# Constant bias in a logarithm, pointer constants in small softmax operations, and the first loads in another order: attention with a rational feed-forward on one core

## The chip, the cores and the metric

One NeuronCore of a Trainium2 chip runs the whole kernel as one program. The metric is the device time of one execution in microseconds; the times given for the kernel before are three runs, and a profile was taken of one further execution. Engines are named as the profile names them: PE (TensorE, with PEld for its weight loads), DVE (VectorE), ACT (ScalarE), POOL (GpSimd) and SP (SyncE, which issues every load and store).

## The reference

Two attentions and a feed-forward layer, on 8 batches of 8 heads, 576 rows of 64 columns:

```
p_packed = softmax(p k^T / 8) v            # 32 packed queries per head
out      = softmax(q p_packed^T / 8) p_packed
x = out as 4608 rows of 512
h = x @ w_in                               # 512 x 2048
g = (a0 + a1 h + a2 h^2 + a3 h^3) / (1 + |b0||h| + |b1| h^2 + 1e-6)
y = g @ w_out                              # 2048 x 512
```

Each softmax divides by its sum plus 1e-9. The weights `w_in` and `w_out` arrive as 64-bit floats and are turned into 32-bit floats on the chip.

## The kernel before

**The work.** The feed-forward is cut into 128 *units*: one batch, one half of its 576 rows, one chunk of 256 of the 2048 hidden columns (`hidden`, L882 on). A unit multiplies on PE into a PSUM tile `h`; ACT makes `U` = |b0 h|, `sq` = b1 h^2 and the first term of the polynomial `Y` from it; DVE continues `Y`; POOL adds `U` and `sq`; ACT takes the logarithm of that sum plus one (`sq<-U,one`, the operation at L905) and the exponential of its negative, which is the reciprocal that divides; two DVE operations finish. Three units later `acc_block` multiplies the result by `w_out` into `acc`. The first 12 units (`PLAIN`) multiply in full 32-bit precision; from the 13th on each operand is split into a high and a low part (`split`, `divide`), with a cast on ACT (`gh`, `half`, `w`) and a subtraction on POOL (`gl`, `w<-w,w 128x512`).

**Weights.** `load_words` loads the 64-bit words in 16 pairs of transfers of 512 KB, in the order in which they fall due: `w_in` chunks 0 to 3 are pairs 1 to 4, `w_out` chunks 0, 1 and 2 are pairs 5, 6 and 7, and pair 8 is `w_in` chunk 4. A pair waits for a free buffer: `m` buffers, or the ring `w`, of which buffers 2 and 3 hold v and q of batch 0 until that attention is done (`started`). `convert` turns a pair into 32-bit floats: two ACT operations of 128x1024 (`w<-w`, `m<-m`, `half<-w`, `win<-w`), two on DVE and a sum on DVE or POOL. `divide` splits a chunk of `w_out` (one cast on ACT, two subtractions of 128x512 on POOL).

**Attention.** `attention(bb)` of batch 0 runs ahead of everything; that of each later batch is spread between the units of the batch before. Its small operations work on a tile `small`: the negated row maximum (128x2, or 128x1 with a pointer), `tot` = sum + 1e-9 (128x2), and in the second softmax a sum + 1e-9 of 128x18.

**The order.** Every operation is recorded by a `Planner` with a cost; it builds the dependencies, simulates the engines with these costs and issues all engines in the order found. So the cost of one operation, or one more dependency, moves operations everywhere. Only the operations recorded before `nc.pin()` (L1005) keep their written order: the list of first loads at L1000. All other transfers, those of `a` and `b` among them (L404, recorded in `constants`), are placed by the planner. Each transfer also waits until the one eight places ahead of it has landed. In gaps of PE the planner's times leave, `idle` puts small products with a tile of zeros (`acc<-w,zero`).

Names in the rows are those of tiles (`kx`, `AH`: attention; `at`, `acc`, `h`: PSUM). All planned instructions have L293 as their line.

Of the kernel before, what the change touches and what calls it, by code (L numbers as in the profile page):

```python
# [13 lines left out]
F32 = mybir.dt.float32  # L14
# [10 lines left out]
P = 128  # L25
# [4 lines left out]
S = 2.0**-40  # L30


class Planner:
# [61 lines left out]
    def cost(self, engine, name, args, kwargs):  # L95
        if engine == "sync":
            return self.DMA_ISSUE
        fixed, per = self.COST[engine]
        if engine == "tensor":
            if name == "transpose" or args[1].dtype == F32:  # L100
                fixed, per = self.TRANSPOSE if name == "transpose" else self.F32
        aps = [x for x in args if isinstance(x, bass.AP)]
        if engine == "scalar":
            fixed += (aps[-1].space == PSUM) * -42 + ("accum_out" in kwargs) * 93 + ("bias" in kwargs) * 93
            per += 0.1 * any(x.ap[-1][0] == 2 for x in aps[:2])
        if engine == "gpsimd" and len(aps) < 3:
            fixed, per = 135, 0.9
        if engine == "vector" and len(aps) > 2 and any(self.columns(x) == 1 for x in aps[1:]):
            fixed += 60
        if engine == "vector" and name == "tensor_scalar":  # L110
            per /= 2
        return fixed + per * self.columns(aps[1] if name.startswith("reduce") else aps[0])
# [24 lines left out]
    def shares(self, engine, calls):  # L137
# [9 lines left out]
        wide = sum(self.columns(x) > 8 for x in aps[1:])  # L147
        return wide > 1 or name in ("tensor_scalar", "tensor_copy")

# [175 lines left out]
def attention_rational_ffn(  # L325
# [46 lines left out]
    make_identity(tc.nc, ident)  # L372
    ab, abS, one, root = (sb.tile([P, n], F32, name=x) for n, x in ((6, "ab"), (7, "abS"), (1, "one"), (5, "root")))
    zero = sb.tile([P, 32], F32R, name="zero")
# [26 lines left out]

    def constants():
        nc.vector.tensor_scalar(zero, ident[:, 0:32], 0.0, None, ALU.mult)
        nc.sync.dma_start(ab[:, 0:4], a.rearrange("(o n) -> o n", o=1).broadcast_to([P, 4]))  # L404
        nc.sync.dma_start(ab[:, 4:6], b.rearrange("(o n) -> o n", o=1).broadcast_to([P, 2]))
        nc.vector.tensor_scalar(abS[:, 0:6], ab, S, None, ALU.mult)
        nc.vector.scalar_tensor_tensor(abS[:, 4:6], abS[:, 4:6], -1.0, abS[:, 4:6], ALU.mult, ALU.max)
        nc.vector.memset(one, (1.0 + 1e-6) * S)

# [125 lines left out]
    def load(bb, what):  # L535
        if bb >= B:
            return
        if what == "rem":
# [83 lines left out]
    def attention(bb):  # L622
# [58 lines left out]
        for r in range(NG):  # L681
# [36 lines left out]
            for x in range(2):  # L718
                nc.vector.reduce_max(mx[:, 2 * x + r : 2 * x + r + 1], t[x], axis=AX.X)
            nc.vector.tensor_scalar(of(nb, r), of(mx, r), -SCALE, None, ALU.mult)  # L720
            for x, (c0, c1) in enumerate(KEYS):
# [9 lines left out]
        else:  # L731
            fs = sm
        nc.vector.scalar_tensor_tensor(tot, fs[:, 0:2], 1e-9, fs[:, 2:4], ALU.add, ALU.add)
        nc.vector.reciprocal(rec, tot)
# [98 lines left out]
        for r in range(NG):  # L833
# [6 lines left out]
            nc.vector.reduce_sum(m2[:, 1, :], sT, axis=AX.X)  # L840
            nc.vector.tensor_scalar(m2[:, 1, :], m2[:, 1, :], 1e-9, None, ALU.add)
            nc.vector.reciprocal(m2[:, 2, :], m2[:, 1, :])
# [39 lines left out]
    def hidden(bb, x, c):  # L882
# [21 lines left out]
        yield  # L904
        nc.scalar.activation(U2, U, AF.Ln, bias=one)  # L905
        nc.scalar.activation(V, U2, AF.Exp, scale=-1.0)
# [92 lines left out]

    for what in ("k0", "k1", "r", "p", "qr", 2, "rv", "v0", "v1", 3, "q0", "q1", 4, 5):  # L1000
        if isinstance(what, int):
            load_words(what)
        else:
            load(0, what)
# [113 lines left out]
```

## Time and profile before

| | |
|---|---|
| three runs | 767.41 us median (766.51 to 767.48) |
| the profiled execution | 767.14 us, span 765.4 us |
| mean granted clock of TensorE | 0.982 of full speed |
| busy share of the span | PE 97%, PEld 74%, DVE 86%, ACT 81%, POOL 61% |
| chain of waits, by engine | PE 84%, ACT 6%, DVE 3%, POOL 3%, issue 2%, DMA 1% |
| bytes moved | 56.39 MB |

The span is cut by what the chain of waits goes through: it says, going back from the last instruction, which engine's work each stretch ended on. PE's busy time is not PE at its peak, since matmuls are pipelined and their ends are modelled. Idle time of an engine that is not on the chain costs nothing by itself.

### The profile page before, as it was taken

Reading aid. Unit: us, or ns where it says so; the run is one execution under the profiler, and the core shown is the slowest. Engines: PE = TensorE matmul, PEld = TensorE weight load, DVE = VectorE, ACT = ScalarE, POOL = GpSimd, SP = SyncE. Lnnn points to the kernel's source line nnn. Section 1 sums busy time; section 2 is a strip of 40 time slices with the busy share of each in tenths; the row PEclk is TensorE's granted clock in tenths of the full one; section 3 lists DMA queues with packets and bytes.
Section 4 is the critical chain, followed back from the end, with each engine's and each line's share of the span. In section 5 each row is a group of like instructions: output and inputs, shape, how many; then the busy total and the mean of one; then the engine's idle time right before and its main releaser. Section 6 shows DMA issues by size and latency. Waiting matters only on the chain.

```text
span 765.4 us, 14423 instructions
## 1 busy us (share of the span) xinstructions
PE 738.8 (97%) x5325; PEld 566.5 (74%) x5325; DVE 658.5 (86%) x1042; ACT 619.6 (81%) x1074; POOL 467.0 (61%) x455
## 2 busy tenths in 40 slices
PE   4679999999999999999999999999999999999997
PEld 3456554678788788778788887778887888778886
DVE  2889999988999779998988879998999788988873
ACT  5689978988887787878786877888787797888882
POOL 0024548986686556756685565856687555866762
PEclk8679999999999999999999999999999999999999
DMA  8994740214701139025602119021901006000001
GB/s 261 293 366 126 199 92 0 63 56 60 107 1 56 43 38 127 2 85 68 99 1 57 37 32 141 2 84 25 118 17 56 28 17 91 1 28 1 28 1 42
DMA packets 156632, 56.39 MB, mean 74 GB/s; under 512 B 126865, under 2 KB 145809, under 8 KB 156561
## 3 DMA queue, kind: packets, MB, share of 16 engines
q1 hardware_dynamic: 156560, 55.46, 33.3%
q8 instruction: 42, 0.69, 0.4%
q14 instruction: 30, 0.24, 0.1%
HBM read 46.01 MB, written 9.44 MB: 72 GB/s over the span
## 4 chain that ended last, share of the span: by engine, by line
PE 84%; ACT 6%; DVE 3%; POOL 3%; issue 2%; DMA 1%; SPq 0%; DVEq 0%; POOLq 0%; ACTq 0%
PE acc L293 43%; PE h L293 25%; PE at L293 15%; DVE Y L293 1%; POOL w L293 1%; ACT sq L293 1%; POOL U L293 1%; ACT U L293 1%; ACT m L293 1%; ACT Y L293 1%; ACT kx L293 1%; POOL gl L293 1%; DVE small L293 1%; ACT w L293 1%; DMA pn<-in_p_dram 1%
## 5 line engine op out<-in xcount | busy, mean ns | idle before, releaser
L293 POOL TENSOR_TENSOR U<-U,sq 128x576 f32<-128x576 f32 x128 | 186.4, 1456 | 141.4 <-ACT sq L293 137.0
L293 DVE SCALAR_TENSOR_TENSOR Y<-Y,abS,h 128x576 f32<-128x576 f32 x256 | 205.8, 805 | 50.6 <-ACT h L293 48.6
L293 PE MATMUL acc<-w,gh 128*128 128x512 f32 x736 | 239.2, 408 | 0.4 <-ACT half L293 0.3
L293 PE MATMUL h<-AH,m 128*128 128x288 f32 x1024 | 194.6, 314 | 0.5 <-DVE Y L293 0.2
L293 POOL TENSOR_TENSOR gl<-Y,gh 128x512 fp32r<-128x512 f32 x116 | 150.2, 1295 | 57.7 <-POOL G L293 18.4
L293 PEld LDWEIGHTS h<-AH,m 128*128 128x128 f32 x1024 | 159.7, 189 | 28.9 <-issue 9.8
L293 PEld LDWEIGHTS acc<-w,gh 128*128 128x128 f32 x736 | 133.4, 188 | 42.5 <-issue 12.3
L293 PE MATMUL acc<-w,gl 128*128 128x512 f32 x384 | 152.7, 416 | 1.3 <-POOL gl L293 1.2
L293 ACT ACTIVATE sq<-U,one 128x576 f32<-128x576 f32 x128 | 100.8, 788 | 34.0 <-POOL U L293 33.4
L293 ACT ACTIVATE U<-h 128x576 f32<-128x576 f32 x128 | 83.4, 651 | 34.9 <-PE h L293 33.8
L293 DVE TENSOR_TENSOR Y<-Y,h 128x576 f32<-128x576 f32 x128 | 95.5, 746 | 14.8 <-ACT Y L293 13.5
L293 ACT ACTIVATE h<-sq 128x576 f32<-128x576 f32 x128 | 84.8, 663 | 18.5 <-DVE Y L293 15.8
L293 ACT ACTIVATE Y<-h,abS 128x576 f32<-128x576 f32 x128 | 96.3, 752 | 0.0
L293 DVE SCALAR_TENSOR_TENSOR h<-U,h 128x576 f32<-128x576 f32 x128 | 96.2, 751 | 0.0
L293 PE MATMUL h<-AL,m 128*128 128x288 f32 x448 | 95.8, 294 | 0.0
L293 PEld LDWEIGHTS acc<-w,gl 128*128 128x128 f32 x384 | 71.8, 188 | 29.3 <-issue 10.5
L293 DVE SCALAR_TENSOR_TENSOR Y<-h,Y 128x576 f32<-128x576 f32 x116 | 87.1, 751 | 1.8
L293 ACT CAST gh<-Y 128x512 fp32r<-128x512 f32 x116 | 72.5, 625 | 19.1 <-DVE Y L293 12.3
L293 ACT ACTIVATE sq<-h 128x576 f32<-128x576 f32 x128 | 83.4, 651 | 0.0
L293 PE MATMUL acc<-half,gh 128*128 128x512 f32 x240 | 79.3, 412 | 0.0
L293 PEld LDWEIGHTS h<-AL,m 128*128 128x128 f32 x448 | 71.8, 188 | 0.1
L293 PEld LDWEIGHTS acc<-half,gh 128*128 128x128 f32 x240 | 43.4, 188 | 13.7 <-issue 5.8
(144 smaller groups left out, 900.8 us busy)
## 6 DMA issues: line engine op xcount, KB each, us to landing
w<-in_moe_w_out_dram SPq DMA_DIRECT2D x16, 512.0 KB, 4.7
out_dram<-half SPq DMA_DIRECT2D x15, 512.0 KB, 3.1
nat<-in_k_dram SPq DMA_DIRECT2D x48, 144.0 KB, 4.1
nat<-in_q_dram SPq DMA_DIRECT2D x48, 144.0 KB, 4.3
nat<-in_v_dram SPq DMA_DIRECT2D x24, 256.0 KB, 3.4
m<-in_moe_w_in_dram SPq DMA_DIRECT2D x10, 512.0 KB, 8.9
w<-in_moe_w_in_dram SPq DMA_DIRECT2D x6, 512.0 KB, 9.2
nat<-in_k_dram SPq DMA_DIRECT2D x4, 512.0 KB, 6.8
```

Source lines behind the costliest of these rows:

```text
L293: getattr(getattr(self.nc, engine), name)(*args, **kwargs)
```

## The change

Five edits. The logarithm's bias is a number instead of a pointer to the one-column tile `one`, which goes. Two columns behind `a` and `b` hold 1e-9 and -1/8, set by POOL; the negated maximum of batches 0 and 1 and the 128x18 sum take their constant from there as a pointer, and `tot` becomes two operations of one column with a pointer. The loads of `a` and `b` go into the fixed list, ahead of q. Pairs 6 and 7 follow pair 5 in the fixed list, into `w` buffers that are free (before, the planner placed them, and they went into the buffers of v and q). The planner's costs follow: a number as bias costs nothing extra, and a `tensor_scalar` with a pointer counts as one column a cycle and as not sharing POOL's port.

```diff
--- before.py
+++ after.py
@@ -101,13 +101,13 @@
                 fixed, per = self.TRANSPOSE if name == "transpose" else self.F32
         aps = [x for x in args if isinstance(x, bass.AP)]
         if engine == "scalar":
-            fixed += (aps[-1].space == PSUM) * -42 + ("accum_out" in kwargs) * 93 + ("bias" in kwargs) * 93
+            fixed += (aps[-1].space == PSUM) * -42 + ("accum_out" in kwargs) * 93 + isinstance(kwargs.get("bias"), bass.AP) * 93
             per += 0.1 * any(x.ap[-1][0] == 2 for x in aps[:2])
         if engine == "gpsimd" and len(aps) < 3:
             fixed, per = 135, 0.9
         if engine == "vector" and len(aps) > 2 and any(self.columns(x) == 1 for x in aps[1:]):
             fixed += 60
-        if engine == "vector" and name == "tensor_scalar":
+        if engine == "vector" and name == "tensor_scalar" and len(aps) == 2:
             per /= 2
         return fixed + per * self.columns(aps[1] if name.startswith("reduce") else aps[0])
 
@@ -145,7 +145,7 @@
         if any(x.space == PSUM for x in aps):
             return False
         wide = sum(self.columns(x) > 8 for x in aps[1:])
-        return wide > 1 or name in ("tensor_scalar", "tensor_copy")
+        return wide > 1 or name in ("tensor_scalar", "tensor_copy") and len(aps) == 2
 
     def mode(self, engine, calls):
 
@@ -370,7 +370,8 @@
 
     ident = sb.tile([P, P], F32, name="ident")
     make_identity(tc.nc, ident)
-    ab, abS, one, root = (sb.tile([P, n], F32, name=x) for n, x in ((6, "ab"), (7, "abS"), (1, "one"), (5, "root")))
+    ab, abS, root = (sb.tile([P, n], F32, name=x) for n, x in ((8, "ab"), (7, "abS"), (5, "root")))
+    ab, eps, minus = ab[:, 0:6], ab[:, 6:7], ab[:, 7:8]
     zero = sb.tile([P, 32], F32R, name="zero")
     win = sb.tile([P, NCH, NCC, CF], F32, name="win")
     G = sb.tile([P, NFC, 2 * REM], F32, name="G")
@@ -400,12 +401,11 @@
 
 
     def constants():
+        nc.gpsimd.memset(eps, 1e-9)
+        nc.gpsimd.memset(minus, -SCALE)
         nc.vector.tensor_scalar(zero, ident[:, 0:32], 0.0, None, ALU.mult)
-        nc.sync.dma_start(ab[:, 0:4], a.rearrange("(o n) -> o n", o=1).broadcast_to([P, 4]))
-        nc.sync.dma_start(ab[:, 4:6], b.rearrange("(o n) -> o n", o=1).broadcast_to([P, 2]))
         nc.vector.tensor_scalar(abS[:, 0:6], ab, S, None, ALU.mult)
         nc.vector.scalar_tensor_tensor(abS[:, 4:6], abS[:, 4:6], -1.0, abS[:, 4:6], ALU.mult, ALU.max)
-        nc.vector.memset(one, (1.0 + 1e-6) * S)
 
         m, e, p, r, i = (root[:, n : n + 1] for n in range(5))
         nc.vector.scalar_tensor_tensor(m, ab[:, 5:6], -1.0, ab[:, 5:6], ALU.mult, ALU.max)
@@ -534,6 +534,10 @@
 
     def load(bb, what):
         if bb >= B:
+            return
+        if what == "ab":
+            nc.sync.dma_start(ab[:, 0:4], a.rearrange("(o n) -> o n", o=1).broadcast_to([P, 4]))
+            nc.sync.dma_start(ab[:, 4:6], b.rearrange("(o n) -> o n", o=1).broadcast_to([P, 2]))
             return
         if what == "rem":
             for x in ("r", "p", "qr", "rv"):
@@ -717,7 +721,7 @@
             )
             for x in range(2):
                 nc.vector.reduce_max(mx[:, 2 * x + r : 2 * x + r + 1], t[x], axis=AX.X)
-            nc.vector.tensor_scalar(of(nb, r), of(mx, r), -SCALE, None, ALU.mult)
+            nc.vector.tensor_scalar(of(nb, r), of(mx, r), minus, None, ALU.mult)
             for x, (c0, c1) in enumerate(KEYS):
                 i = slice(2 * x + r, 2 * x + r + 1)
                 nc.scalar.activation(KX[:, r, c0:c1], t[x], AF.Exp, bias=nb[:, i], scale=SCALE, accum_out=sm[:, i])
@@ -730,7 +734,8 @@
             nc.vector.tensor_mul(fs, f, sm)
         else:
             fs = sm
-        nc.vector.scalar_tensor_tensor(tot, fs[:, 0:2], 1e-9, fs[:, 2:4], ALU.add, ALU.add)
+        for r in range(NG):
+            nc.vector.tensor_scalar(tot[:, r : r + 1], fs[:, r : r + 1], eps, fs[:, 2 + r : 3 + r], ALU.add, ALU.add)
         nc.vector.reciprocal(rec, tot)
         if rows4(bb):
             nc.vector.tensor_mul(xr(F), xr(f), two(rec))
@@ -838,7 +843,7 @@
             nc.scalar.activation(sT, sT, AF.Exp, scale=SCALE)
             yield
             nc.vector.reduce_sum(m2[:, 1, :], sT, axis=AX.X)
-            nc.vector.tensor_scalar(m2[:, 1, :], m2[:, 1, :], 1e-9, None, ALU.add)
+            nc.vector.tensor_scalar(m2[:, 1, :], m2[:, 1, :], eps, None, ALU.add)
             nc.vector.reciprocal(m2[:, 2, :], m2[:, 1, :])
             eng.tensor_mul(sT, sT, bc(2))
             if bb == 0:
@@ -902,7 +907,7 @@
         nc.vector.scalar_tensor_tensor(Y, Y, a1, V, ALU.add, ALU.mult)
         nc.gpsimd.tensor_add(U, U, U2)
         yield
-        nc.scalar.activation(U2, U, AF.Ln, bias=one)
+        nc.scalar.activation(U2, U, AF.Ln, bias=(1.0 + 1e-6) * S)
         nc.scalar.activation(V, U2, AF.Exp, scale=-1.0)
         nc.vector.scalar_tensor_tensor(Y, Y, a0, V, ALU.add, ALU.mult)
         nc.vector.scalar_tensor_tensor(V, U, (1.0 + 1e-6) * S, V, ALU.add, ALU.mult)
@@ -997,7 +1002,7 @@
         elif i == 1:
             nc.sync.dma_start(ov, o)
 
-    for what in ("k0", "k1", "r", "p", "qr", 2, "rv", "v0", "v1", 3, "q0", "q1", 4, 5):
+    for what in ("k0", "k1", "r", "p", "qr", 2, "rv", "v0", "v1", 3, "ab", "q0", "q1", 4, 5, 6, 7):
         if isinstance(what, int):
             load_words(what)
         else:
```

**The loads.** On SP's queue, from v of batch 0 on (`w_1`: v, `w_2`: q, `m_3`, `m_4`: pairs 3 and 4, `w_3`: pair 5; `nat`, `AH_2`, `pn_2`: batch 1), before:

```order
L293 DMA w_1_82<-in_v_dram 128x4x256 x2
L293 DMA m_3_83<-in_moe_w_in_dram 128x2x256 x2
L293 DMA w_2_84<-in_q_dram 128x4x256 x2
L293 DMA m_4_85<-in_moe_w_in_dram 128x2x256 x2
L293 DMA w_3_86<-in_moe_w_out_dram 128x512 x2
L293 DMA ab<-in_moe_b_dram 128x2
L293 DMA nat_3_106<-in_k_dram 128x4x256
L293 DMA ab<-in_moe_a_dram 128x4
L293 DMA AH_2_108<-in_k_dram 64x8x64
```

and now:

```order
L293 DMA w_1_81<-in_v_dram 128x4x256 x2
L293 DMA m_3_82<-in_moe_w_in_dram 128x2x256 x2
L293 DMA ab<-in_moe_a_dram 128x4
L293 DMA ab<-in_moe_b_dram 128x2
L293 DMA w_2_83<-in_q_dram 128x4x256 x2
L293 DMA m_4_84<-in_moe_w_in_dram 128x2x256 x2
L293 DMA w_3_85<-in_moe_w_out_dram 128x512 x2
L293 DMA w_4_86<-in_moe_w_out_dram 128x512 x2
L293 DMA w_5_87<-in_moe_w_out_dram 128x512 x2
L293 DMA nat_3_107<-in_k_dram 128x4x256
```

`a` and `b` stand ahead of q; pairs 6 and 7 (`w_4_86`, `w_5_87`) stand ahead of batch 1's k, where before they followed ten transfers of batch 1.

**ACT ahead of the first unit.** From the last copies of batch 0's first products (`m_7`) to the first unit's `U`, before:

```order
L293 COPY m_7_134<-at_17_135 128x256
L293 ACTIVATE root<-root 128x1
L293 COPY m_7_134<-at_18_136 128x256
L293 ACTIVATE root<-root 128x1
L293 TENSOR_LOAD abS x2
L293 ACTIVATE w_4_119<-w_4_119 128x1024
L293 TENSOR_LOAD abS
L293 COPY kx_2_141<-at_19_143 128x512
L293 COPY kx_2_141<-at_20_144 128x512
L293 ACTIVATE w_8_132<-w_4_119 128x1024
L293 ACTIVATE U_1_126<-h_1_127 128x576
```

and now:

```order
L293 COPY m_7_133<-at_17_134 128x256
L293 COPY m_7_133<-at_18_135 128x256
L293 ACTIVATE w_4_86<-w_4_86 128x1024
L293 ACTIVATE w_8_131<-w_4_86 128x1024
L293 ACTIVATE w_5_87<-w_5_87 128x1024
L293 ACTIVATE half_1_156<-w_5_87 128x1024
L293 COPY kx_2_140<-at_19_142 128x512
L293 COPY kx_2_140<-at_20_143 128x512
L293 ACTIVATE U_1_125<-h_1_126 128x576
```

The square root's operations (`root`) and the register loads from `abS` moved ahead; the conversion of pair 7 (`w_5`, `half_1`) moved in front of the first unit, beside that of pair 6 (`w_4`).

**POOL around the 9th to 14th unit.** `w_17` to `w_19` 128x512 are subtractions of `divide`, `U_9` and so on the units' sums; before:

```order
L293 TENSOR_TENSOR U_9_219<-U_9_219,sq_9_222 128x576
L293 TENSOR_TENSOR U_10_231<-U_10_231,sq_10_234 128x576
L293 TENSOR_TENSOR U_11_238<-U_11_238,sq_11_241 128x576
L293 TENSOR_TENSOR kx_2_141<-kx_2_141,small 128x576
L293 TENSOR_TENSOR w_17_254<-w_15_226,w_17_254 128x512
L293 TENSOR_TENSOR kx_2_141<-kx_2_141,small 128x576
L293 TENSOR_TENSOR U_12_250<-U_12_250,sq_12_253 128x576
L293 TENSOR_TENSOR w_17_254<-w_15_226,w_17_254 128x512
L293 TENSOR_TENSOR w_16_246<-w_14_215,w_16_246 128x1024
L293 TENSOR_TENSOR w_19_276<-w_16_246,w_19_276 128x512
```

and now:

```order
L293 TENSOR_TENSOR U_9_218<-U_9_218,sq_9_221 128x576
L293 TENSOR_TENSOR w_18_259<-w_15_225,w_18_259 128x512 x2
L293 TENSOR_TENSOR w_19_275<-w_16_245,w_19_275 128x512
L293 TENSOR_TENSOR U_10_230<-U_10_230,sq_10_233 128x576
L293 TENSOR_TENSOR kx_2_140<-kx_2_140,small 128x576
L293 TENSOR_TENSOR w_19_275<-w_16_245,w_19_275 128x512
L293 TENSOR_TENSOR kx_2_140<-kx_2_140,small 128x576
L293 TENSOR_TENSOR U_11_237<-U_11_237,sq_11_240 128x576
L293 TENSOR_TENSOR w_16_245<-w_14_198,w_16_245 128x1024
```

Four of the subtractions now stand ahead of `U_11`, where before none did (two others, `half_6`, stood between units 7 and 9 and now stand behind unit 2).

## Rows read from the trace of the kernel before

**Rows 1.** Busy time by stretch: start and end in us, length, then busy us (and instructions) of PE, PEld, DVE, ACT and POOL, the granted clock of TensorE, the busy share of the DMA engines, GB/s.

```profile
0.00:48.50 48.50, 28.34 (x301) 19.66 (x301) 30.85 (x70) 31.64 (x59) 4.59 (x11) 0.78 0.96 293
48.50:114.50 66.00, 65.93 (x441) 38.10 (x446) 62.22 (x97) 59.05 (x98) 29.36 (x16) 0.95 0.61 172
114.50:158.70 44.20, 43.09 (x255) 25.20 (x254) 42.69 (x70) 38.90 (x63) 40.51 (x35) 1.00 0.14 39
158.70:765.00 606.30, 601.39 (x4338) 483.58 (x4338) 522.75 (x809) 490.02 (x856) 392.50 (x395) 1.00 0.27 48
```

**Rows 2.** Pieces of the chain of waits: start in us, length in us, engine and tile written.

```profile
66.40 2.10 PE acc L290 x24
...
123.81 4.59 POOL w L293 x3
...
158.68 2.11 PE acc L293 x8
```

**Rows 3.** Shares of the chain by engine and tile in the stretch 48.5 to 114.5 us.

```profile
by line: PE acc L293 47.0%; PE h L293 27.4%; PE at L293 19.5%; PE acc L290 6.0%; issue 0.1%
```

**Rows 4.** The same for the stretch 114.5 to 158.7 us.

```profile
by line: POOL w L293 22.8%; issue 14.2%; POOL U L293 9.6%; DVE Y L293 7.0%; ACT sq L293 6.2%; ACT Y L293 5.7%; POOL gl L293 5.6%; ACT U L293 5.3%; ACT w L293 4.5%; ACT m L293 4.5%; ACT h L293 2.7%; ACT half L293 2.4%; POOL kx L293 2.1%; DVE
```

**Rows 5.** The same for the stretch 158.7 to 765 us.

```profile
by line: PE acc L293 48.9%; PE h L293 28.0%; PE at L293 15.8%; DVE Y L293 1.2%; ACT sq L293 0.9%; issue 0.7%; ACT U L293 0.5%; POOL U L293 0.5%; POOL gl L293 0.4%; ACT m L293 0.4%; ACT Y L293 0.3%; DVE kx L293 0.3%; DVE h L293 0.2%; ACT h L
```

**Rows 6.** ACT in order of time: start us, duration us, operation, shapes, and in brackets the idle time before it and what ended that.

```profile
36.83 0.25 ACT L293 ACTIVATE root<-root 128x1 f32<-128x1 f32 x1
...
40.93 1.19 ACT L293 ACTIVATE w<-w 128x1024 f32<-128x1024 f32 x1 [3.49 <-DMA w<-in_moe_w_out_dram]
42.02 1.05 ACT L293 COPY kx<-at 128x512 f32<-128x512 f32 x2
42.96 1.18 ACT L293 ACTIVATE w<-w 128x1024 int32<-128x1024 uint32 x1
44.01 0.66 ACT L293 ACTIVATE U<-h 128x576 f32<-128x576 f32 x1
...
56.27 0.65 ACT L293 ACTIVATE U<-h 128x576 f32<-128x576 f32 x1 [0.88 <-PE h L293]
```

**Rows 7.** DVE in order of time, same columns: the two last transposes of batch 0's attention.

```profile
36.32 0.77 DVE L293 STREAM_TRANSPOSE AH<-kx 128x576 f32<-128x576 f32 x1
...
40.65 0.77 DVE L293 STREAM_TRANSPOSE AH<-kx 128x576 f32<-128x576 f32 x1
```

**Rows 8.** SP's transfers in order of time: start us, time in which they were issued, tile and source, number of transfers.

```profile
15.82 1.50 SPq L293 DMA_DIRECT2D w<-in_q_dram  x2
...
19.97 1.14 SPq L293 DMA_DIRECT2D w<-in_moe_w_out_dram  x2
21.52 1.03 SPq L293 DMA_DIRECT2D ab<-in_moe_b_dram  x1
...
24.42 0.33 SPq L293 DMA_DIRECT2D ab<-in_moe_a_dram  x1
...
34.73 1.97 SPq L293 DMA_DIRECT2D w<-in_moe_w_out_dram  x2
36.95 0.89 SPq L293 DMA_DIRECT2D w<-in_moe_w_in_dram  x2
```

**Rows 9.** Groups by form: operation, shapes, count, busy us and mean ns of one, idle time before.

```profile
L293 ACT ACTIVATE sq<-U,one 128x576 f32<-128x576 f32 x128 | 100.8, 788 | 34.0 <-POOL U L293 33.4
L293 ACT ACTIVATE Y<-h,abS 128x576 f32<-128x576 f32 x128 | 96.3, 752 | 0.0
...
L293 ACT ACTIVATE U<-h 128x576 f32<-128x576 f32 x128 | 83.4, 651 | 34.9 <-PE h L293 33.8
...
L293 POOL TENSOR_TENSOR w<-w,w 128x512 fp32r<-128x512 f32 x10 | 12.8, 1287 | 0.4 <-ACT w L293 0.4
...
L293 DVE TENSOR_SCALAR small<-small 128x18 f32<-128x18 f32 x16 | 7.0, 436 | 0.0
...
L293 DVE SCALAR_TENSOR_TENSOR small<-small 128x2 f32<-128x2 f32 x8 | 3.3, 408 | 0.0
...
L293 DVE TENSOR_SCALAR small<-small 128x1 f32<-128x1 f32 x12 | 2.5, 206 | 0.1
```

**Rows 10.** DVE in order of time: small operations between 60 and 135 us.

```profile
61.84 1.37 DVE L293 TENSOR_SCALAR small<-small 128x2 f32<-128x2 f32 x1
...
67.72 0.16 DVE L293 TENSOR_SCALAR small<-small 128x2 f32<-128x2 f32 x1
...
72.62 1.39 DVE L293 SCALAR_TENSOR_TENSOR small<-small 128x2 f32<-128x2 f32 x1
...
126.10 1.35 DVE L293 TENSOR_SCALAR small<-small 128x18 f32<-128x18 f32 x1
...
132.94 0.94 DVE L293 TENSOR_SCALAR small<-small 128x18 f32<-128x18 f32 x1
```

**Rows 11.** POOL in order of time: sums `U` and three subtractions of `divide`.

```profile
61.29 1.90 POOL L293 TENSOR_TENSOR U<-U,sq 128x576 f32<-128x576 f32 x1
...
71.95 2.04 POOL L293 TENSOR_TENSOR U<-U,sq 128x576 f32<-128x576 f32 x1 [2.19 <-ACT sq L293]
...
123.77 4.88 POOL L293 TENSOR_TENSOR w<-w,w 128x512 fp32r<-128x512 f32 x3
```

## Prediction made before the run

> **What bounds the kernel now.** I read busy time by stretch first, then the chain of waits, since the first shows where the engines are full and the second which of them a stretch ended on. Four stretches come out [rows 1]. Up to 48.5 us the loads fill the DMA engines (0.96 of their time) and no engine is full. From 48.5 to 114.5 us the chain is PE's alone, and 6.0% of it, 4.0 us, are products with the zero tile, which stand where PE has nothing ready [rows 3]; one block of them alone is 2.10 us [rows 2]. From 114.5 to 158.7 us the chain leaves PE: POOL's subtractions of the divided weights hold 22.8%, its other work 17% more, ACT's six operations of a unit with the conversions 31% [rows 4]; DVE is busy 42.7 of 44.2 us, POOL 40.5, ACT 38.9 [rows 1]. The wait ends with PE's `acc` at 158.68 [rows 2]. From there on PE holds 92.7% of the chain, and only 7.3% of 606 us, 44 us, pass through other engines [rows 5]. So what an edit saves on ACT or DVE is worth little after 158.7 us, something between 114.5 and 158.7, and its start in the first 48 us is worth what the first unit gains.
>
> **The front.** The first unit's `U` stands on ACT at 44.01 us. Ahead of it ACT sat 3.49 us until `w_out` landed at 40.93 and then spent 3.1 us on pair 6 and two copies [rows 6]. That is pair 6, issued at 34.73 because ten transfers of batch 1 and those of `a` and `b` went ahead [rows 8]. In the fixed list it is issued right behind pair 5 (19.97) and lands some 6 to 8 us before ACT asks for it. ACT then waits for no load at 37.44 (40.93 − 3.49), but now has four conversions there instead of two: start to start 42.02 − 40.93 = 1.09 and 44.01 − 42.96 = 1.05, so four are 4.3, and two copies 0.94: 42.7 us. The unit also needs the last transpose of the attention, at 40.65 plus 0.77 [rows 7], and then four products on PE; q comes some 0.4 us later behind `a` and `b` (two more places in the queue), so `U` can start at about 42.9. That is **−1.1 us**. Bounds: −3.5, the whole wait on ACT, if the conversions were free, and +1.8 if batch 1's k, now behind 2 MB more of weights, holds PE between the products of the first two units for the time of one more transfer (512 KB at the stretch's mean of 293 GB/s [rows 1] are 1.8 us). The root's operations, which stood between the transposes, go ahead into time in which DVE waits; I give nothing for them, since ACT's queue decides.
>
> **The logarithm.** 128 operations read `one` and take 788 ns. The price of a pointer as bias shows in two operations with the same source and shape: `Y<-h,abS` with one, 752, `U<-h` without, 651 [rows 9]. So 101 ns each, 12.9 us of ACT in all. Eighteen units have their logarithm before 158.7 us: 1.8 us there; 110 after it: 11.1 us. What hides them is PE. If ACT were the bound throughout, all 12.9 would be gained; if PE, nothing.
>
> **The pointers.** A small DVE operation takes 0.16 us when POOL is idle and 1.37 or 1.39 us when it starts under a sum of POOL's that began just before [rows 10, 11]. The sums with 18 columns average 436 ns over 16, `tot` 408 over 8, while the 12 that read their second number through a pointer average 206 [rows 9]. Between 60 and 135 us four of them took 1.37 + 1.39 + 1.35 + 0.94 = 5.05 us [rows 10], 4.4 more than 0.16 each. I take it that with a pointer they do not wait. Nothing in the trace shows a pointer operation with an even number of columns and both sides in SBUF, so both ends are open: 4.4 us less on DVE, or none. `tot` as two operations costs 2 × 0.2 against 0.408, nothing.
>
> **The move on POOL.** Because pairs 6 and 7 are there early and the planner holds ACT cheaper, four of `divide`'s subtractions stand ahead of `U_11` which stood behind it, at 1.29 us each [rows 9]: 5.1 us leave the stretch from 114.5 us on, where three in a row held 4.88 us [rows 11], for one in which POOL is busy 29.4 of 66 us [rows 1].
>
> **Sum for 48.5 to 158.7 us.** The three savings lie on three engines side by side, so I weight each by its engine's share of the chain [rows 4]: POOL 0.40 × 5.1 = 2.0; ACT 0.31 × 1.8 = 0.6; DVE, with 7.0% shown and at most 7.4% in the cut-off rest, 0.14 × (1.35 + 0.94 − 0.32) = 0.3. In PE's stretch I take a third of the 4.0 us of zero products as gained, since POOL and DVE have less in front of what PE waits for there: 1.3; no row splits these 4.0, so both ends, 0 and 4.0, go into the bounds. Together **−4.2 us**. Bounds: 0, where what is won on one engine is waited for on the next, and −9.1, all of POOL's 5.1 and all the 4.0.
>
> **After 158.7 us.** An ACT operation shorter by 0.1 us shortens each unit's chain from `h` to the last DVE operation; 7.3% of the time it is that chain that counts: 0.073 × 11.1 = 0.8, and the rest of the pointer waits about 0.2. **−1.0 us**. Bounds: −6, half of ACT's saving, if the planner uses it to close gaps elsewhere, and +3, if the new order makes one more stretch in which PE is behind the others.
>
> Sum: −1.1 − 4.2 − 1.0 = −6.3 us on the profiled execution's 767.14, so 760.8; the median of the runs is 0.27 above it: **761.1 us**.
>
> **Rivals.**
>
> *The even pointers still wait.* Small operations with 18 and 2 columns would go on waiting for POOL, and only `tot`, split into single columns, would not. Then DVE's 0.3 and 0.2 of the sum fall away, and the planner, which now holds these operations as not sharing, puts them under POOL's sums more often: one or two more waits of 1.2 us (1.37 − 0.16) where DVE is fullest, 1.5 us. That is 763.1 us. For it: the 1.37 us row is an operation with a number [rows 10], and none with a pointer and an even count is there to compare. Against it: the pointer rows' mean of 206 ns has no long one among them. The Trainium skill ("SBUF — State Buffer", section Who interferes with whom) counts `tensor_scalar` among the operations that can take the port pair shared with GpSimd, if its operands allow the two-port mode, and names no exception for a pointer; by it this rival would hold for the 18 columns. No row here shows such an operation with a pointer.
>
> *Hidden.* PE's products between 48.5 and 114.5 us are the same in number, and from 158.7 us they fill 92.7% of the chain. If the early lead is eaten where PE waits for its PSUM banks and the late stretches fall as they did before, only the front's 1.1 us stays: 766.3 us, not told from no change. I count the change as told from none where it is over 0.2% (1.5 us), about what a measurement of this kernel can tell.
>
> *Slower: ACT's queue behind the second unit.* Between the second unit's logarithm and the third unit's `U` ACT now has five conversions and a cast of `divide` (1.07 each), the second unit's exponential and two exponentials of batch 1 with their sums (estimated 2.0 together): 8.4 us. It reaches that point some 7 us behind the first `U` (ten operations of 0.65 to 0.79 [rows 9]), near 49.7, so the third `U` stands at 58.1 instead of 56.27 [rows 6]: 1.8 us later, and PE's third unit with it. The first of these conversions is pair 8, whose transfers were issued at 36.95 [rows 8] and now stand behind v of batch 1, which waits for a buffer that PE frees only when it has transposed batch 1's k. If pair 8 lands late, everything listed waits in ACT's queue: 3.5 us, by the wait at 40.93 [rows 6]. DVE and POOL wait for the same exponentials, so their parts of the sum come to nothing: −1.1 + 1.8 + 3.5 − 0.6 for the logarithm = +3.6 on 767.4, **771.0 us**. It decides from the point where pair 8 lands after 53 us. Against it: ACT asks for it only near 50, 13 us after its old issue.
>
> *A larger gain.* If DVE is what truly fills 60 to 158 us, the pointers and the idle time closed by early conversions count in full: −9.1 there and −3 later, 755 us.
>
> **How the numbers follow.** Forecast 0.52 (756 to 765); still waiting 0.10 (763); hidden 0.15 (766.3); slower 0.17 (771); larger gain 0.06 (755). Faster by over 0.2% (under 765.9): 0.52 + 0.10 + 0.06 = 0.68; within 0.2%: 0.15; slower: 0.17. The range reaches from 755.5, near the larger gain, to 768.5, over the hidden case and the mildest of the slower one; it leaves out some 0.05 below and 0.13 above.
>
> **What the profile after would show.** ACT's first wait for `w_out` gone and the first `U` near 43 us; `sq<-U` at about 690 ns; the sums of 18 columns at about 170 to 200 ns, with no one over 0.5 us; fewer zero products; the chain's return to PE near 153 to 154 us instead of 158.7; the stretch after it within 2 us of 606. I am wrong if `U` of the first unit is no earlier, if small operations with a pointer still show 0.9 to 1.4 us, if the third unit's `U` comes after 60 us, or if the time from the return to PE to the end has changed by more than the front has.

## The result, and the profile after

The change made the kernel slower: 773.86 us, median of 6 runs (772.37 to 775.20), against 767.44 (766.51 to 769.82) for the kernel before beside it. The ratio is 1.0093, 95% interval 1.0080 to 1.0105 (the two medians alone give 1.0084). Forecast were 761.1 us, in a range from 755.5 to 768.5. The profiled execution took 772.71 us, its span is 770.9.

**Busy time by stretch**, change; columns as in [rows 1], which it answers to:

```profile
0.00:48.50 48.50, 28.18 (x301) 18.96 (x301) 29.84 (x68) 32.83 (x58) 3.88 (x12) 0.79 0.85 276
48.50:114.50 66.00, 62.69 (x417) 34.90 (x418) 63.13 (x99) 58.59 (x100) 33.43 (x21) 0.92 0.63 185
114.50:158.70 44.20, 43.52 (x239) 26.07 (x238) 41.51 (x69) 37.58 (x63) 36.88 (x31) 1.00 0.13 39
158.70:765.00 606.30, 600.93 (x4334) 482.67 (x4333) 529.10 (x815) 480.38 (x855) 391.96 (x395) 1.00 0.26 47
```

Two things are new. In the second stretch PE is idle for 3.3 us and its mean granted clock is lower than in [rows 1]; in the last, PE is idle for 5.4 us, all of it before 745 us. In the kernel before it is idle for 1.2 us there. From 158.7 to 745 us, the kernel before and then the change:

```profile
158.70:745.00 586.30, 585.09 (x4267) 470.42 (x4268) 514.80 (x798) 484.25 (x847) 385.72 (x389) 1.00 0.28 48
```

```profile
158.70:745.00 586.30, 580.93 (x4238) 465.67 (x4237) 518.60 (x801) 471.38 (x840) 380.81 (x384) 1.00 0.27 48
```

**The front**, change. Transfers as in [rows 8], then ACT as in [rows 6]:

```profile
13.92 0.47 SPq L293 DMA_DIRECT2D ab<-in_moe_a_dram  x1
14.62 0.35 SPq L293 DMA_DIRECT2D ab<-in_moe_b_dram  x1
15.01 1.06 SPq L293 DMA_DIRECT2D w<-in_q_dram  x2
...
19.53 8.29 SPq L293 DMA_DIRECT2D w<-in_moe_w_out_dram  x6
28.91 1.71 SPq L293 DMA_DIRECT2D nat<-in_k_dram  x2
...
44.47 1.02 SPq L293 DMA_DIRECT2D w<-in_moe_w_in_dram  x2
```

```profile
39.23 3.22 ACT L293 ACTIVATE w<-w 128x1024 f32<-128x1024 f32 x3
42.31 1.19 ACT L293 ACTIVATE half<-w 128x1024 int32<-128x1024 uint32 x1
43.61 1.07 ACT L293 COPY kx<-at 128x512 f32<-128x512 f32 x2
45.51 0.65 ACT L293 ACTIVATE U<-h 128x576 f32<-128x576 f32 x1 [0.82 <-PE h L293]
...
53.31 1.16 ACT L293 ACTIVATE w<-w 128x1024 f32<-128x1024 f32 x1
...
61.16 0.65 ACT L293 ACTIVATE U<-h 128x576 f32<-128x576 f32 x1
```

Six `w_out` transfers go out in one piece. Batch 1's k follows at 28.91 (22.99 before), pair 8 at 44.47 (36.95 [rows 8]). ACT's wait for `w_out` is gone, as forecast, but the first `U` stands at 45.51 and the third at 61.16 (44.01 and 56.27 [rows 6]). What stood ahead of the first `U`, on PE and DVE of the change:

```profile
25.40 1.94 PE L293 MATMUL at<-ident,w 128*128 128x128 f32 x8 [2.52 <-DMA w<-in_q_dram]
...
42.23 0.78 DVE L293 STREAM_TRANSPOSE AH<-kx 128x576 f32<-128x576 f32 x1
...
42.87 1.14 PE L293 MATMUL at<-ident,nat 128*128 128x128 f32 x8
```

PE waited 2.52 us for q, which the kernel before did not, the last transpose came at 42.23 (40.65 [rows 7]), and eight transposes of batch 1's k stood ahead of the unit's last products.

**TensorE's granted clock**, 50 to 65 us: three stretches of the kernel before, then of the change. The third number from the right is the clock; 1.00 is 2.4 GHz, 0.50 is 1.2 GHz.

```profile
50.00:55.00 5.00, 4.97 (x15) 2.98 (x14) 3.63 (x7) 4.87 (x9) 0.79 (x1) 0.54 1.04 388
55.00:60.00 5.00, 5.00 (x41) 3.29 (x40) 3.32 (x6) 4.12 (x7) 2.46 (x2) 1.00 1.06 372
60.00:65.00 5.00, 5.00 (x12) 1.90 (x10) 5.00 (x7) 5.00 (x11) 3.18 (x2) 1.00 0.33 77
```

```profile
50.00:55.00 5.00, 3.82 (x34) 2.53 (x34) 5.00 (x6) 4.57 (x9) 2.41 (x2) 0.50 1.06 372
55.00:60.00 5.00, 3.94 (x7) 2.34 (x8) 4.12 (x11) 5.00 (x7) 2.53 (x2) 0.50 1.06 373
60.00:65.00 5.00, 5.00 (x40) 3.24 (x39) 4.77 (x8) 4.75 (x12) 2.56 (x2) 0.99 1.10 319
```

Before, PE is busy all but throughout 50 to 55 us and the clock is back at 1.00 from 55 on. In the change PE has gaps from 47 to 56 us, and the clock comes back at 60. The gaps, of the kernel before and then of the change:

```profile
48.54 1.97 PE L293 MATMUL at<-ident,nat 128*128 128x128 f32 x8 [4.03 <-ACT m L293]
```

```profile
48.73 0.66 PE L293 MATMUL at<-ident,nat 128*128 128x128 f32 x4 [1.70 <-ACT m L293]
50.20 1.12 PE L293 MATMUL at<-ident,nat 128*128 128x128 f32 x4 [0.81 <-ACT m L293]
...
53.48 1.32 PE L293 MATMUL at<-kx,small 64*32 64x256 f32 x24 [0.78 <-ACT small L293]
56.06 2.08 PE L293 MATMUL acc<-w,gh 128*128 128x512 f32 x2 [1.25 <-DVE gh L293]
```

Both kernels lose about as much in gaps, 4.0 and 4.5 us. In the kernel before it is one gap that ends at 48.54; in the change there are four, the last of which ends at 56.06. None of them ends on a transfer: PE waits for copies of ACT and for `gh` of DVE.

**What PE waits for**, change (total us, times, longest):

```profile
PE h L293 <- DVE Y L293: 4.6, 10, 0.9
...
PE at L293 <- DMA w<-in_q_dram: 2.5, 1, 2.5
...
PE acc L293 <- DVE gh L293: 1.3, 1, 1.3
```

In the kernel before the first of these was:

```profile
PE h L293 <- DVE Y L293: 0.2, 1, 0.2
```

The ten lie between 167 and 671 us. The chain from 158.7 to 765 us shows the same, where [rows 5] had almost PE alone:

```profile
by line: PE acc L293 30.0%; PE h L293 19.3%; DVE Y L293 14.4%; PE at L293 9.8%; issue 4.2%; DVE h L293 3.8%; DVE small L293 3.5%; DVE kx L293 3.3%; ACT h L293 1.7%; ACT sq L293 1.5%; DVE m L293 1.2%; POOL gl L293 1.1%; ACT U L293 1.0%; POOL
```

One of the ten waits, DVE and then PE, change:

```profile
497.28 0.73 DVE L293 SCALAR_TENSOR_TENSOR h<-U,h 128x576 f32<-128x576 f32 x1
497.92 0.68 DVE L293 TENSOR_TENSOR m<-at,m 128x512 fp32r<-128x512 f32 x1
498.52 0.74 DVE L293 SCALAR_TENSOR_TENSOR Y<-h,Y 128x576 f32<-128x576 f32 x1
```

```profile
499.41 0.76 PE L293 MATMUL h<-AH,m 128*128 128x288 f32 x4 [0.89 <-DVE Y L293]
```

DVE works without a gap, and `Y`, which makes room for PE's next `h`, has its place behind an operation of `m` and work of the attention.

**Where the time went, by progress.** I count PE's busy time without the zero products (5.46 us before, 2.21 after) backwards from the end and look when each kernel has the same work left. Against the kernel before the change is 4.8 us behind at 60 us, 1.3 at 160, 4.2 at 420, 5.5 at 700. So there are two losses, one in the front, most of which is taken up by 160 us, and one spread over the rest. A single trace gives the front only roughly: two experiments below, e7 and e8, have the same order, and their first `U` stand at 47.10 and 44.44, their lag at 60 us is 4.5 and 0.8.

**Small operations**, change: DVE's sum of 18 columns with the pointer, alone and under POOL's sums, and POOL at the third of them:

```profile
121.63 0.23 DVE L293 TENSOR_SCALAR small<-small,ab 128x18 f32<-128x18 f32 x1
...
125.13 1.21 DVE L293 TENSOR_SCALAR small<-small,ab 128x18 f32<-128x18 f32 x1
...
490.95 1.32 DVE L293 TENSOR_SCALAR small<-small,ab 128x18 f32<-128x18 f32 x1
```

```profile
490.81 1.43 POOL L293 TENSOR_TENSOR U<-U,sq 128x576 f32<-128x576 f32 x1 [1.61 <-ACT sq L293]
```

The operation starts 0.14 us into POOL's sum and ends with it, pointer or not. The groups by form, which answer to [rows 9]:

```profile
L293 ACT ACTIVATE sq<-U 128x576 f32<-128x576 f32 x128 | 88.8, 693 | 34.8 <-POOL U L293 34.5
...
L293 DVE TENSOR_SCALAR small<-small,ab 128x18 f32<-128x18 f32 x16 | 11.4, 712 | 0.0
...
L293 DVE TENSOR_SCALAR small<-small,ab 128x1 f32<-128x1 f32 x16 | 4.1, 268 | 0.0
```

### The profile page after: what moved, and what is told of

It reads as the page before. It is cut to its first block, busy times and chain, and to the rows that moved or that the text cites. A ratio compares the mean times of both kernels' runs of the same rounds, so it can differ in the third digit from the quotient of the medians.

```text
span 770.9 us, 14377 instructions
## 1 busy us (share of the span) xinstructions
PE 737.1 (96%) x5296; PEld 563.7 (73%) x5296; DVE 664.5 (86%) x1049; ACT 610.0 (79%) x1074; POOL 466.1 (60%) x457
## 4 chain that ended last, share of the span: by engine, by line
PE 58%; DVE 24%; ACT 7%; DMA 4%; issue 4%; POOL 2%; SPq 1%; DVEq 0%; ACTq 0%; POOLq 0%
PE acc L293 29%; PE h L293 19%; DVE Y L293 12%; PE at L293 10%; DVE small L293 3%; DVE h L293 3%; DVE kx L293 3%; ACT h L293 1%; ACT sq L293 1%; DMA w<-in_q_dram 1%; DVE m L293 1%; ACT U L293 1%; ACT Y L293 1%; DMA w<-in_moe_w_out_dram 1%; DMA m<-in_moe_w_in_dram 1%
## 5 line engine op out<-in xcount | busy, mean ns | idle before, releaser
L293 DVE SCALAR_TENSOR_TENSOR Y<-Y,abS,h 128x576 f32<-128x576 f32 x256 | 205.7, 804 | 52.5 <-ACT h L293 50.2
L293 PEld LDWEIGHTS acc<-w,gh 128*128 128x128 f32 x736 | 133.7, 188 | 45.4 <-issue 11.4
L293 ACT ACTIVATE sq<-U 128x576 f32<-128x576 f32 x128 | 88.8, 693 | 34.8 <-POOL U L293 34.5
```

Source lines behind the costliest of these rows:

```text
L293: getattr(getattr(self.nc, engine), name)(*args, **kwargs)
```

## Experiments

All ratios are to the kernel before, with 95% intervals. The theories have letters: A, the pointers; B, the loads; C, any new order of the program is a draw (chance decides whether it is a good one) worth some us; D to F, narrower forms with the planner's price for the logarithm; G, pairs 6 and 7 delay the clock.

### One part at a time, and two by two

**e1_log.** `bias=one` becomes `bias=(1.0 + 1e-6) * S` in the logarithm, with the planner's price:

```
-... + ("bias" in kwargs) * 93
+... + isinstance(kwargs.get("bias"), bass.AP) * 93
```

> The kernel before with the logarithm's bias as a number alone, and the planner's price for it with it; loads, pointers and the rest as before. Theory A (what the change lost, it lost on DVE through the pointers) and theory B (it lost it in the front, through the loads): neither holds for this kernel, so 766 to 767.4 us, at most 1.5 us faster, with the logarithm at 690 ns. Theory C (any other input to the planner gives another order of the whole program, and orders differ by a few us whatever the edit): the time may come out anywhere between 764 and 771.

Measured 766.83 us, 0.9998 (0.9986 to 1.0011). With the logarithm alone the time is the same; what its order drew is in that, and can't be taken apart here.

**e2_pointers.** The pointers alone, with their planner lines:

```
-nc.vector.tensor_scalar(m2[:, 1, :], m2[:, 1, :], 1e-9, None, ALU.add)
+nc.vector.tensor_scalar(m2[:, 1, :], m2[:, 1, :], eps, None, ALU.add)
...
-return wide > 1 or name in ("tensor_scalar", "tensor_copy")
+return wide > 1 or name in ("tensor_scalar", "tensor_copy") and len(aps) == 2
```

> The kernel before with the pointers alone (18 columns, 2 columns, tot in single columns) and the planner's rules that go with them. Theory A: the 16 operations with 18 columns average about 0.7 us as in the change, against 0.44 with a number, PE shows some ten waits for DVE's Y between 160 and 700 us, and the time is about 4 us over the kernel before: 771 us. Theory B: the operations may wait, but PE doesn't, and the time stays at 767.4 within 1.5 us. Theory C: 764 to 771.

Measured 766.69 us, 0.9998 (0.9986 to 1.0009); the 18 columns average 435 ns, as with a number [rows 9]. A falls: in this order the pointers cost nothing.

**e3_loads.** The loads alone:

```
-... "v0", "v1", 3, "q0", "q1", 4, 5):
+... "v0", "v1", 3, "ab", "q0", "q1", 4, 5, 6, 7):
```

> The kernel before with the loads alone: a and b ahead of q, pairs 6 and 7 behind 5. Theory B: it holds nearly the whole loss, 772 to 774 us, with q's transposes near 25.4 us, the third unit's U near 61 us and PE idle for 3 us between 48.5 and 80 us. Theory A: the same lateness up to 80 us, but 2 us of it come back by 160 us as in the change, so 768.5 to 769.5. Theory C: 764 to 771.

Measured 770.36 us, 1.0037 (1.0023 to 1.0050), with no wait for `Y` at all: two fifths of the change's loss, more than A said, less than B, and inside C's range. It stays behind to the end: 6.5 us at 60 us, 3.5 at 160, 4.6 at 700.

**e4_nine.** The change with 18 = 2 × 9:

```
-nc.vector.tensor_scalar(m2[:, 1, :], m2[:, 1, :], eps, None, ALU.add)
+for y in range(0, 2 * NB, NB):
+    nc.vector.tensor_scalar(m2[:, 1, y : y + NB], m2[:, 1, y : y + NB], eps, None, ALU.add)
```

> The change with each sum of 18 columns cut into two of 9, both with the pointer, so that their number of columns is odd as in tot's operations, which never waited. Theory A: none of the 32 lasts over 0.3 us, DVE's waits for POOL there are gone, PE's ten waits for Y go to two or three, and the time falls by about 4 us to 770. Theory B: the same operations, but the time stays at 773 to 774. Theory C: the planner sees other costs here too, so 770 to 777.

Measured 776.42 us, 1.0119 (1.0103 to 1.0135), a clear miss. The 32 operations average 566 ns, so nine columns wait for POOL too; 32 of them hold DVE 17.3 us instead of 11.4, and PE's waits for `Y` rise to 7.7 us. How much of the 2.6 us over the change is theirs isn't shown, since the order is another one too.

**e5_log_pointers, e6_log_loads, e7_pointers_loads** combine the edits above two by two.

> Logarithm and pointers together, loads as before. Either of them alone cost nothing. Theory D (the two together tighten DVE: ACT's shorter unit moves POOL's sums onto DVE's small operations, the planner holds the pointers as free of POOL, and PE waits for DVE's Y): 770 us, 3 us over the kernel before, with some ten waits for Y and the sums of 18 columns near 0.7 us. Theory B (only the loads cost, and what the change lost beyond them belongs to them too): 766.5 to 767. Theory C (each order differs by chance): 765 to 770, with no tie between the mean of those sums and the time.

> Logarithm and loads together, small operations as before. Theory D: the loads' 3.4 us alone, 770.4. Theory E (it is the logarithm with the loads: ACT, shorter by 0.1 us a unit, lets the planner set its late start off against DVE): 773 to 774, with some ten waits for Y. Theory C: 768 to 773.

> Pointers and loads together, the logarithm's bias as before through a pointer. Theory D: the loads' 3.4 us alone, 770.4, with no wait for Y over 0.5 us after 160 us. Theory A again (pointers cost as soon as the front is late): 773 to 774. Theory C: 768 to 773.

Measured 770.86 us, 1.0052 (1.0039 to 1.0064); 772.95, 1.0082 (1.0068 to 1.0095); 767.60, 1.0013 (1.0004 to 1.0022). Logarithm and pointers, each worth nothing, together cost 4 us; loads cost 3.4 alone and 0.7 with the pointers. The edits' costs don't add. D's time fits e5 alone, with 18 columns at 669 ns as it asked, but five waits for `Y` (1.6 us) where it asked for ten; E comes near e6, with three waits. C missed too: e5 is 0.9 us over the highest that it gave, e7 0.4 us under the lowest. But e7 is nearly 3 us under D, and C is the theory that comes nearest to all three.

**e8_old_price.** The change, with the planner's price for a bias put back to `("bias" in kwargs) * 93`.

> The change with one line undone: the planner holds the logarithm at its old price, with 93 ns for a bias, while the chip runs it with the number. Theory D in its narrow form (the planner's new price for ACT makes the tight order, not the instruction): 770.4 us, PE without waits for Y, the logarithm still at 690 ns. If the shorter instruction itself does it: 773 to 774. Theory C: 768 to 773.

Measured 767.89 us, 1.0010 (0.9999 to 1.0021): 6 us less than the change, from one number of the planner. D in its narrow form gave 770.4, the shorter instruction 773 to 774, and C's range begins 0.1 us higher. The instructions of e8 come in the same order as those of e7, save one memset of 0.06 us that e7 has more, and only the logarithm differs. e7's row, then e8's:

```profile
L293 ACT ACTIVATE sq<-U,one 128x576 f32<-128x576 f32 x128 | 100.6, 786 | 37.1 <-POOL U L293 36.8
```

```profile
L293 ACT ACTIVATE sq<-U 128x576 f32<-128x576 f32 x128 | 88.8, 694 | 37.1 <-POOL U L293 36.7
```

So 11.8 us less on ACT, in the same order, are worth 767.60 − 767.89 = −0.3 us, give or take about 1.1 by the two intervals: nothing that can be told. This order has one wait for `Y` after 160 us, where the change has ten:

```profile
PE h L293 <- DVE Y L293: 0.9, 1, 0.9
```

### Is it the price's direction, or a draw?

**e9_price31, e10_price62, e11_price124, e12_price155.** The change, with `("bias" in kwargs) * 31`, 62, 124, 155.

> The change with the planner's price for the logarithm's bias at 31 ns instead of 0 (the change) or 93 (e8); instructions, loads and pointers as in the change. Theory F (the price acts in one direction: the cheaper the planner holds ACT, the later DVE's results come to PE): between 0 and 93, so about 772 us. Theory C (the price only deals another order, and orders of the same instructions differ by some us either way): anywhere from 766 to 775, in no row with the other prices.

> The same with a price of 62 ns. Theory F: about 770 us, between the price of 31 and that of 93. Theory C: anywhere from 766 to 775.

> The same with a price of 124 ns, over that of the kernel before. Theory F: not over 767.9 us, the time at 93, and 766 if the trend goes on. Theory C: anywhere from 766 to 775.

> The same with a price of 155 ns. Theory F: not over the time at 124, 765 to 767 us. Theory C: anywhere from 766 to 775.

Measured 775.85 us, 1.0131 (1.0116 to 1.0145); 770.48, 1.0060 (1.0047 to 1.0072); 771.68, 1.0070 (1.0057 to 1.0083); 768.48, 1.0040 (1.0027 to 1.0052). In row of prices 0, 31, 62, 93, 124, 155: 0.93%, 1.31, 0.60, 0.10, 0.70, 0.40 over the kernel before. That goes up, down and up again: F falls, C stands, with one order 0.9 us beyond its range. The same instructions in six orders spread over 1.2%, 9 us.

**e15_before_price62, e16_before_price124.** The kernel before, all its instructions, with a price of 62 and 124 for 93.

> The kernel before, all its instructions, loads and operands, with the planner's price for a bias at 62 ns instead of 93: another order and nothing else. If orders differ by chance and the kernel before is one of the lucky ones: 768 to 773 us, the clock rising near 54 us all the same. If its order is typical and the spread belongs to the change: 766 to 768.

> The same with a price of 124 ns. A lucky order of before: 768 to 773 us. A typical one: 766 to 768. In both cases no wait of PE for q's load.

Measured 769.59 us, 1.0044 (1.0028 to 1.0060), and 769.67, 1.0046 (1.0032 to 1.0060). The kernel before is the best of three orders of its own instructions. In e16 PE waits 0.26 us for q, where none was expected.

### Which half of the loads

**e13_ab_early, e14_pairs_early**: the kernel before, with `..., 3, "ab", "q0", "q1", 4, 5` and with `..., "q0", "q1", 4, 5, 6, 7`.

> The kernel before with a and b among the first loads, ahead of q, and pairs 6 and 7 where they were. If a and b make the late clock (q waits behind them: PE idle 1.5 to 2.5 us for q near 25 us): the clock rises for good at 60 us or later and the time is 769 to 771 us. If the pairs make it: PE may wait for q, but the clock rises near 54 us and the time is 766 to 768, within what another order gives.

> The kernel before with pairs 6 and 7 in the fixed list behind 5, and a and b where they were. If the pairs make the late clock (batch 1's k lands behind 2 MB more, so PE has its transposes and the third unit later): the clock rises for good at 60 us or later, the third unit's U stands near 60 us and the time is 769 to 772 us. If a and b make it: the rise near 54 us, and 766 to 768.

Measured 769.54 us, 1.0049 (1.0030 to 1.0068), and 773.34, 1.0089 (1.0074 to 1.0104). The clock as above, 50 to 65 us, e13 and then e14:

```profile
50.00:55.00 5.00, 4.61 (x13) 3.28 (x14) 4.97 (x10) 5.00 (x8) 0.57 (x1) 0.50 1.05 356
55.00:60.00 5.00, 5.00 (x23) 3.45 (x21) 1.12 (x3) 3.52 (x7) 3.26 (x2) 0.96 0.88 282
```

```profile
50.00:55.00 5.00, 0.64 (x24) 0.35 (x18) 4.38 (x7) 5.00 (x7) 3.13 (x2) 0.81 1.04 387
55.00:60.00 5.00, 1.83 (x24) 0.84 (x24) 4.34 (x10) 5.00 (x10) 2.70 (x3) 0.50 1.06 379
60.00:65.00 5.00, 4.04 (x12) 2.86 (x13) 5.00 (x12) 4.98 (x10) 2.67 (x2) 0.50 1.10 349
```

The pairs make the late clock, a and b don't: with them PE waits 0.44 us for q in e13. In e14 batch 1's k is issued at 29.71 and its transposes are done before 48.2; PE, which has little to do from 50 us on, stands twice for the softmax of batch 1 behind conversions in ACT's queue:

```profile
55.46 1.83 PE L293 MATMUL at<-kx,small 64*32 64x256 f32 x24 [4.82 <-ACT kx L293]
60.96 1.33 PE L293 MATMUL at<-ident,kx 128*128 128x128 f32 x5 [3.67 <-ACT kx L293]
```

Both times lie 1.3 to 1.5 us over what was expected of them; e13 has nearly the clock of the kernel before and is one more order at 0.5%.

**e17_no_pairs, e18_ab_late**: the same two halves taken out of the change.

> The change without pairs 6 and 7 in the fixed list, which end with pair 5 as before; a and b stay ahead of q, logarithm and pointers as in the change. Theory G (batch 1's k behind 2 MB of weights makes TensorE's clock rise for good 5 us or more later, and that is the 3 to 4 us that the loads cost; the rest of the difference between two kernels is the lot of the order): k of batch 1 issued near 24 us, rise at 56 us or before, 767 to 771 us. If a and b make it: rise at 60 us or later and 771 to 775.

> The change with a and b fetched where the kernel before fetches them, pairs 6 and 7 in the fixed list. Theory G: k of batch 1 issued near 29 us, rise at 60 us or later, 770 to 776. If a and b make it: rise at 56 us or before, 767 to 771.

Measured 772.71 us, 1.0077 (1.0058 to 1.0096), and 777.01, 1.0123 (1.0108 to 1.0139). Issue of k and clock came as G said: 22.64 us and full by 55 in e17, 30.19 us, 0.50 until 62.5 and 0.58 from there to 65 in e18. e17's time lies 1.7 us over what G gave it, with 4.2 us of waits for `Y` in eight pieces, which I read as an unlucky order; by its time alone it would fit the other side (771 to 775). e18 is 1 us over G's range.

### All kernels together

| kernels | issue of batch 1's k, us | first `U`, us | clock back over 0.95 from, us | over the kernel before |
|---|---|---|---|---|
| pair 5 last: before, e1, e2, e5, e13, e15, e16, e17 | 22.6 to 24.8 | 42.3 to 44.7, mean 43.8 | 52.5 to 57.5 | −0.02 to 0.77%, mean 0.33% |
| pair 7 last: change, e3, e4, e6 to e12, e14, e18 | 27.6 to 30.4 | 44.0 to 47.4, mean 45.7 | 60 to 67.5 | 0.10 to 1.31%, mean 0.78% |

(e7 and e8, one order, count once in the last mean.) The clock is read in windows of 2.5 us. Its column does not overlap between the groups, in 20 kernels, nor does that of k, which the edit itself puts off. Two kernels fall once more, and they are the two slowest by the ratio: e9 to 0.71 and 0.60 in the two windows from 162.5 to 167.5 us, after one with PE busy for 1.83 of 2.5 us, and e18 to 0.62 and 0.70 from 675 to 680, after 1.19 of 2.5; about 1.7 us each.

The means of the times are 0.45% apart, with a standard error of 0.16% (from the spread of 8 and 11 orders): 3.5 us, give or take 2.4. The four couples that differ in the pairs alone give 0.89% (before, e14), −0.12 (e13, e3), 0.16 (e17, change) and 0.71 (e5, e18), 0.41 on average. Counted by progress, the lower group is on average 5.8 us behind the upper at 60 us, 3.1 at 160 and 4.1 at 700 (standard errors of 1.1, 0.9 and 1.3, one trace each): most of the pairs' loss is there by 160 us. Between 45 and 80 us 35 × (1 − mean granted clock), which is what the half clock takes if PE has work all that time, averages 2.6 us in the upper row and 5.1 in the lower. By that the clock is 2.5 of the 5.8 us at 60; what it is of the 3.5 at the end isn't shown. e8 and e12 have the late clock and are 0.10 and 0.40% over the kernel before.

By which way the pairs make it late isn't separated either. They put off batch 1's k, and they also bring their conversions to ACT earlier. In all 20 kernels every gap of PE between 44 and 62 us that ends on a wait ends on ACT or DVE, none on a transfer, and in e14 conversions stand in front of what PE waits for. No run loads the pairs early and converts them late.

## Why the prediction was wrong

In terms of the table: pairs 6 and 7 cost about 0.45%, 3.5 us; the kernel before stands 0.33%, 2.5 us, better than the mean of its group, and the change 0.15%, 1.2 us, worse than that of its own. Together 0.93%. This adds up averages over orders; in the change's own trace 1.3 of 5.5 us are there at 160 us and the rest comes where PE waits for `Y`. That its instructions need not cost this much is shown by e8, the same instructions in another order, at 0.10%. No share is shown to need the logarithm or the pointers themselves, beyond the order that the planner makes of their prices.

- **The front: wrong, and the first step that failed.** The first `U` was to come at 42.9 and came at 45.51. ACT's wait for `w_out` went away as said, but the way over q and PE was mis-sized: q was to come 0.4 us later, a figure for which no row stood, and PE waited 2.52 us for it; the last transpose, taken as fixed at 40.65, came at 42.23, and k's transposes came ahead of the products. For batch 1's k I gave 1.8 us as a bound; it was 6 us on the issue (28.91 for 22.99). The other term that I put at nothing is PE's clock, which my sum held as given: PE's gaps lasted to 56 us instead of 48.5, and the clock stayed at 0.50 to 60 us instead of 55.
- **The logarithm: duration right, place wrong by its size.** 693 ns for 690, 12 us of ACT. I gave it 0.6 + 0.8 us of the time; e8 against e7 gives −0.3, give or take 1.1, and from 115 to 160 us both make up the same 2.4 us against the kernel before.
- **The pointers: wrong.** The 18 columns go on waiting for POOL, up to 1.37 us, and alone take 0.23 us for 0.17. It is the rival's mechanism: the Trainium skill ("SBUF — State Buffer", section Who interferes with whom) counts `tensor_scalar` among the operations that can contend with POOL, if their operands allow the mode that takes both ports, and the trace agrees for a pointer as for a number. Of an operand the Trainium skill ("VectorE: DVE Perf Modes", section Mode 2×_2P) asks for an even outermost count or an odd one that is equal on both sides, for that mode; the 566 ns of nine columns agree as far as a wait goes, and no row shows the mode itself. Single columns never waited: 267 to 271 ns on average wherever they were run. The rows with 206 ns, from which I took it that a pointer does not wait [rows 9], are of single columns too. That tot's split gained is still not shown, 2 × 0.268 against 0.408 [rows 9]. Over all orders the 18 columns average 0.32 to 0.64 us with a number and 0.44 to 0.74 with a pointer; the rival's price, 1.5 us, is not told by any run, since the order decided the time.
- **The move on POOL, and 48.5 to 158.7 us: right in direction, no use.** POOL has 36.9 us of work there instead of 40.5, the chain is back on PE at 133.2 us, and of 4.8 us lag 3.5 are made up by 160. But e14, with neither logarithm nor pointers, makes up more (9.5 at 60 us, 4.6 at 160). The stretch has slack that takes a late front up; I had booked that slack as gain.
- **After 158.7 us: wrong, by more than its bound.** Forecast −1.0, at worst +3; it was +4.2. PE waits for `Y` in ten places, 4.6 us. The step that failed is not a duration; it is that I priced edits one by one in a program whose whole order is planned anew. Six orders of one set of instructions spread over 9 us, more than the sum of all my terms.
- **The slower rival** (third `U` at 58.1, pair 8 late, 771.0) had the place and came nearest in time, and half of its mechanism is there. Between the second unit's logarithm and the third `U` ACT works off just the operations that it listed, without a gap, from 53.31 to 61.16: 7.85 us for 8.4. It comes to them 3.6 us later than the rival had it (49.7). ACT does not wait for pair 8, whose 3.5 us fall away, so that the sum comes near is in part luck.

What stays open: why a given order ends with PE waiting for `Y`. Waits of 4 us and more go with times in the upper half of their group (e4, e9, e17, e18, the change), but e14 and e6 are there with 1.7 and 2.3 us of them. Whether a and b ahead of q cost something of their own can't be told from an order's draw; PE's wait for q, 0 to 2.6 us with them and at most 0.3 without, is all that the traces show of it. No version that beats the kernel before was found.

## What to carry to other kernels

Where a planner sets the order from its prices, an edit's own cost has to be taken at one order, as e8 against e7; a comparison of two planned programs measures two draws as well, so deal several orders of both before believing a few tenths of a per cent. A load that is moved ahead can cost more than it saves: here PE ran dry later in the front, and its clock came back later, whether by the next batch's k that was put off or by the conversions that came early. And what DVE loses to POOL depends on when it starts, not on where its second operand comes from.

## What the runs showed of the hardware

- The clock comes back later than the work: in e14, PE is busy for 2.5 of the 10 us from 50 to 60, its clock falls to 0.50 (1.2 GHz), and it is still at 0.50 from 60 to 65 us although PE is then busy for 4.04 of 5; from 67.5 on it is 1.00 (2.4 GHz).
- A [128, 1] `tensor_scalar` with two pointers took 0.27 us whatever POOL did; nine columns waited like eighteen. So did two columns at times: 0.16 us alone with a number, 1.37 under a sum of POOL's [rows 10].
- A pointer costs 60 ns on an undisturbed DVE operation of 18 columns (0.23 for 0.17 us) and 92 ns on ACT's logarithm (786 for 694 ns).
